# The first 26 units of a Fourier-transform and feed-forward kernel: another order of weight conversion, other engines for input folds and products

## The chip, the cores and the metric

The kernel runs on one core of a Trainium2 chip. The metric is the device time of one execution in microseconds (us). One core has five engines with an instruction stream each: TensorE (PE, matrix products; its weight loads are listed as PEld), VectorE (DVE), ScalarE (ACT), GpSimd (POOL) and SyncE (SP), which here issues the DMA transfers. Each engine takes its instructions in the order in which they are written; semaphores order the engines among each other. Data lies in SBUF (on-chip memory), results of TensorE in PSUM, which is divided into eight banks of 128 partitions x 512 float32.

## The reference

```python
X = np.fft.fft(x, axis=1)            # x: 8 x 3008 x 256 float32
X = np.fft.fft(X, axis=2)
x = X.real.astype(np.float32).reshape(24064, 256)
h = x @ w_in                         # w_in: 256 x 2048, float64
g = np.where(h >= 1, h, np.where(h <= -1, 0.0, (h + 1) ** 2 / 4))
out = (g @ w_out).astype(np.float32) # w_out: 2048 x 256, float64
```

The real part of a two-dimensional Fourier transform of each of 8 batches goes through a feed-forward layer: a product with w_in, a function that is quadratic between -1 and 1, a product with w_out.

## The kernel before

**Transform.** The sequence axis, 3008 = 47 x 64, is transformed in two stages of matrix products with small constant matrices (cs). A batch comes in 8 pieces (x_b_q, 512 KB each). A piece is *folded* (fold_x, L131: the sum y of its two halves), then multiplied (stage1_sums, L291, s1), copied into z (stage1_copy, L309), and after all 8 pieces six stage-2 sums follow (stage2_sums, L352, s2). Each s2 piece is *split* into a rounded high part pqh (ScalarE) and the rest pql (VectorE) (split, L165). Two s2 pieces make the columns of one of three chunks k. The transform along the last axis is folded into w_in: fold_w_in (L264) multiplies converted w_in by the constant matrix cm (wps) and ScalarE stores the high part wh; fold_low (L280) stores the low part wl on VectorE. One row of it is kept apart as delta (spread_delta, copy_delta, move_delta).

**Weights.** float64 is not a type of the chip, so each weight tile n (0 to 15, 128 x 512 values) is read as integer words and rebuilt as float32: convert_fields (a: mantissa and exponent, two VectorE instructions), convert_floats (b: three on ScalarE), convert_join (c: two on VectorE), convert_scale (d: the product of both on GpSimd; v: the same on VectorE). Tiles 4j and 4j+1 are quarter j of w_in, tiles 4j+2 and 4j+3 are tiles 2j and 2j+1 of w_out (wo_j holds the two).

**Feed-forward.** The work is cut into units (b, k, f): 128 of the 2048 inner columns for one chunk of one batch. Units 0 to 11 are f = 0 to 3 for k = 0, 1, 2 of batch 0; units 12 to 23 are f = 4 to 15 for k = 0. gemm1(i) (L392) makes six matmuls into two PSUM tiles uv; VectorE forms us and h (L404 to L407), ScalarE a (L410, L411). activate(i) (L414) forms g on VectorE (L419); up to unit 23 it stays float32 and gemm2(i) (L437) adds g @ w_out into four accumulators acc with unsplit w_out. In the loop over i, gemm1(i) and activate(i-1) are followed by the steps of the table, and by gemm2 of the unit i-2, from i = 14 on i-4, since gemm2 is left out at i = 8 and 13. From unit 24 on g and w_out are split in high and low parts (u and O make those of w_out) and GpSimd forms g's low part.

**Order.** What comes first is written out by hand: the string START (L67) and the table STEPS (L72) name, by a letter and a number, what is issued at the start and behind gemm1 of each unit up to 26. The letters: l a weight load, k and m the loads of cs and cm, x the load of an input piece, y and g its fold on VectorE and GpSimd, p the sums of stage 1 (p0 to p7), of the Nyquist row (p8) and of stage 2 (p9 to p14 are s2 pieces 0 to 5), z and w copies of s1 into z (z on ScalarE alone, w in halves on both), q the split of an s2 piece (q9 to q14), a b c d v the conversion, f the fold of w_in, s its low part, e and E delta, n the Nyquist row's load, u and O the split of w_out, L and Y load and fold of batch 1's pieces, i and j matmuls on constants that keep TensorE busy. pin (L538) ties every engine to this order up to unit 23.

**PSUM.** Three banks serve uv, four acc0 to acc3, one "fft". While acc is not in use yet, the transform of batch 0 takes the acc banks in turn:

```python
    def fft_bank(b, name):                              # L158
        if b == 0 and early[0] < EARLY_BANKS:
            early[0] += 1
            return ps.tile([P, CH], F32, tag=f"acc{early[0] % 4}", name=name, bufs=1)
        return ps.tile([P, CH], F32, tag="fft", name=name, bufs=1)
```

The first EARLY_BANKS requests go to the acc banks, all later ones to the one "fft" bank, where each waits until the one before it has been read.

Of the kernel before, what the change touches and what calls it, by code (L numbers as in the profile page):

```python
# [113 lines left out]
def fft_ffn_kernel(ctx: ExitStack, tc: tile.TileContext, x, cst, w_in, w_out, out):  # L114
# [16 lines left out]
    def fold_x(b, q, engine=None):  # L131

        t = xt.pop((b, q))
        y = sb.tile([96, CH], F32, tag="y", name=f"y_{b}_{q}", bufs=3)
        (engine or nc.gpsimd).tensor_tensor(y, t[:96, 0], t[:96, 1], op=ALU.add)  # L135
# [127 lines left out]

    def fold_w_in(n):  # L264
        f4, m = divmod(n, 2)
        cols = slice(f4 * CH, (f4 + 1) * CH)
# [4 lines left out]
        for h in range(2):
            nc.tensor.matmul(pt, mats[m][h], f32s[4 * f4 + h], start=(h == 0), stop=(h == 1))  # L272
        nc.scalar.activation(wh[m][:, cols], pt, AF.Copy, scale=inner if m else 1.0)
# [4 lines left out]
        folds[n] = pt

    def fold_low(n):  # L280
        f4, m = divmod(n, 2)
        cols = slice(f4 * CH, (f4 + 1) * CH)
        high = wh[m][:, cols].bitcast(F32)
        if m == 1:
            nc.vector.scalar_tensor_tensor(wl[m][:, cols], folds.pop(n), inner, high, op0=ALU.mult, op1=ALU.subtract)  # L285
# [358 lines left out]
```

## Time and profile before

| | us |
|---|---|
| median of 3 runs (1757.78 to 1761.95) | 1759.48 |
| the profiled execution | 1761.39 |
| its span in the trace | 1759.5 |
| PE busy in the span | 1736.8 |
| VectorE busy | 1427.5 |
| ScalarE busy | 1338.1 |
| GpSimd busy | 1149.9 |

The span runs from the first to the last recorded instruction of the profiled execution; some 1.9 us of its time lie around it. Busy time is the time in which an engine worked on an instruction, and the rest of the span is idle time, of which the trace says what ended it. A row of a timeline such as `36.12 3.47 PE L460 MATMUL acc<-g,wo ... x8 [1.56 <-DVE g L419]` reads: at 36.12 us TensorE began eight matmuls of line 460, which took 3.47 us together, after 1.56 us of idle time that ended when VectorE had finished g. The granted clock is the share of full speed that TensorE was given.

### The profile page before, as it was taken

The numbers are of one execution on the slowest core, as the hardware profiler recorded it, in microseconds if no ns is written. First come the engines' busy times: TensorE is split into PE (matmuls) and PEld (weight loads), VectorE is DVE, ScalarE is ACT, GpSimd is POOL, SyncE is SP. The second block draws the span as 40 slices with busy tenths as digits, with TensorE's granted clock in tenths as the row PEclk, the third lists the DMA queues.
The fourth block names the chain that finished last, engine by engine and source line by source line (L and its number), as shares of the span: only waits on it lengthen the run. The fifth ranks groups of instructions, "written<-read, shape, count | busy, mean of one in ns | idle before, by whom it ended". The sixth has DMA issues, their size and how long they took to land.

```text
span 1759.5 us, 21528 instructions
## 1 busy us (share of the span) xinstructions
PE 1736.8 (99%) x7822; PEld 1393.5 (79%) x7822; DVE 1427.5 (81%) x1753; ACT 1338.1 (76%) x1564; POOL 1149.9 (65%) x800
## 2 busy tenths in 40 slices
PE   8999999999999999999999999999999999999998
PEld 6545788888888888888888888888888878887876
DVE  6998788788887887887887788877888788888886
ACT  6776877787777777787777877778778777777775
POOL 1103757876678766677667776677667766667766
PEclk9999999999999999999999999999999999999999
DMA  8104311110011100111001100111001001000000
GB/s 313 47 24 142 107 66 60 37 60 30 1 60 51 45 30 13 60 58 33 24 13 60 59 31 25 42 42 59 19 25 37 1 24 42 1 25 19 5 24 24
DMA packets 33738, 80.89 MB, mean 46 GB/s; under 512 B 4704, under 2 KB 9952, under 8 KB 33632
## 3 DMA queue, kind: packets, MB, share of 16 engines
q1 hardware_dynamic: 33596, 79.52, 13.1%
q8 instruction: 61, 1.00, 0.2%
q14 instruction: 45, 0.37, 0.1%
q10 hardware_dynamic: 36, 0.01, 0.0%
HBM read 51.70 MB, written 27.81 MB: 45 GB/s over the span
## 4 chain that ended last, share of the span: by engine, by line
PE 56%; ACT 17%; DVE 10%; POOL 9%; issue 7%; DMA 0%; ACTq 0%; SPq 0%; POOLq 0%; DVEq 0%
PE acc L460 35%; PE uv L401 17%; POOL gl L428 8%; DVE h L422 7%; ACT a L411 6%; ACT gh L425 5%; ACT a L410 4%; PE s L298 2%; PE s L364 2%; DVE h L406 1%; DVE h L407 1%; ACT z L321 1%; DMA cm<-in_cst_dram 0%; DVE us L404 0%; PE wps L272 0%
## 5 line engine op out<-in xcount | busy, mean ns | idle before, releaser
L428 POOL TENSOR_TENSOR gl<-h,gh 128x512 fp32r<-128x512 f32 (+1 forms) x720 | 1033.6, 1458 | 447.1 <-ACT gh L425 416.8
L422 DVE SCALAR_TENSOR_TENSOR h<-a,h 128x1024 f32<-128x1024 f32 (+1 forms) x360 | 547.1, 1520 | 225.1 <-ACT a L411 223.7
L425 ACT ACTIVATE gh<-h 128x1024 fp32r<-128x1024 f32 (+1 forms) x360 | 376.7, 1046 | 347.2 <-DVE h L422 306.5
L460 PE MATMUL acc<-gh,woh 128*128 128x512 f32 (+1 forms) x1440 | 570.2, 396 | 3.6 <-DVE o L471 2.2
L460 PE MATMUL acc<-gl,woh 128*128 128x512 f32 (+1 forms) x1440 | 563.8, 392 | 0.9 <-POOL gl L428 0.9
L460 PE MATMUL acc<-gh,wol 128*128 128x512 f32 (+1 forms) x1440 | 560.8, 389 | 0.0
L410 ACT ACTIVATE a<-h,biases 128x1024 f32<-128x1024 f32 (+1 forms) x384 | 432.3, 1126 | 39.9 <-DVE h L407 38.1
L411 ACT ACTIVATE a<-a 128x1024 f32<-128x1024 f32 (+1 forms) x384 | 399.5, 1040 | 7.7
L460 PEld LDWEIGHTS acc<-gh,woh 128*128 128x128 f32 x1440 | 270.7, 188 | 62.3 <-DVE o L471 5.6
L460 PEld LDWEIGHTS acc<-gl,woh 128*128 128x128 f32 x1440 | 271.3, 188 | 58.6 <-POOL gl L428 2.2
L401 PE MATMUL uv<-pqh,wh 128*128 128x512 f32 (+1 forms) x768 | 310.6, 404 | 5.6 <-DVE h L407 2.7
L460 PEld LDWEIGHTS acc<-gh,wol 128*128 128x128 f32 x1440 | 270.7, 188 | 54.7
L406 DVE TENSOR_TENSOR h<-us,uv 128x512 f32<-128x512 f32 (+1 forms) x384 | 259.8, 677 | 62.4 <-POOL gl L428 18.8
L401 PE MATMUL uv<-pqh,wl 128*128 128x512 f32 (+1 forms) x768 | 299.5, 390 | 0.8 <-DVE wl L285 0.8
L401 PE MATMUL uv<-pql,wh 128*128 128x512 f32 (+1 forms) x768 | 299.6, 390 | 0.0
L404 DVE SCALAR_TENSOR_TENSOR us<-nyb,delta,uv 128x512 f32<-128x512 f32 (+1 forms) x384 | 279.2, 727 | 17.8 <-PE uv L401 17.2
L407 DVE TENSOR_TENSOR h<-us,uv 128x512 f32<-128x512 f32 (+1 forms) x384 | 256.4, 668 | 0.0
L401 PEld LDWEIGHTS uv<-pqh,wh 128*128 128x128 f32 x768 | 144.2, 188 | 50.1 <-DVE h L407 8.4
L401 PEld LDWEIGHTS uv<-pqh,wl 128*128 128x128 f32 x768 | 144.5, 188 | 34.2 <-issue 5.0
L401 PEld LDWEIGHTS uv<-pql,wh 128*128 128x128 f32 x768 | 144.4, 188 | 30.3 <-DVE pql L167 0.4
L135 POOL TENSOR_TENSOR y<-x 96x512 f32<-96x512 f32 x59 | 103.8, 1762 | 62.4 <-DMA x<-in_x_dram 40.7
L460 PE MATMUL acc<-g,wo 128*128 128x482 f32 (+1 forms) x192 | 86.2, 591 | 3.3 <-DVE g L419 2.3
(64 smaller groups left out, 687.4 us busy)
## 6 DMA issues: line engine op xcount, KB each, us to landing
x<-in_x_dram SPq DMA_DIRECT2D x64, 512.0 KB, 3.5
out_dram<-o SPq DMA_DIRECT2D x26, 512.0 KB, 2.8
out_dram<-o SPq DMA_DIRECT2D x14, 482.0 KB, 2.9
nyb<-nyr SPq DMA_DIRECT2D x24, 256.0 KB, 3.2
raw<-in_moe_w_in_dram SPq DMA_DIRECT2D x4, 512.0 KB, 6.7
raw<-in_moe_w_out_dram SPq DMA_DIRECT2D x4, 512.0 KB, 10.5
part<-o SPq DMA_DIRECT2D x4, 512.0 KB, 3.1
os<-part SPq DMA_DIRECT2D x4, 512.0 KB, 6.1
```

The source lines that it names most:

```text
L135: (engine or nc.gpsimd).tensor_tensor(y, t[:96, 0], t[:96, 1], op=ALU.add)
L298: nc.tensor.matmul(pt[:, i], y[:, i * P : (i + 1) * P], bm[:96, :], start=True, stop=True)
L401: nc.tensor.matmul(t[:, :n], w[m][:, cols], r[:, m, :n], start=(j == 0), stop=(j == 2))
L404: nc.vector.scalar_tensor_tensor(us, nyb[b, k][:, :n], delta[:, f : f + 1], uv[0], op0=ALU.mult, op1=ALU.add)
L406: nc.vector.tensor_tensor(h[:, 0], us, uv[1], op=ALU.subtract)
L407: nc.vector.tensor_tensor(h[:, 1], us, uv[1], op=ALU.add)
L410: nc.scalar.activation(a, h, AF.Relu, bias=half, scale=0.5)
L411: nc.scalar.activation(a, a, AF.Square)
L422: nc.vector.scalar_tensor_tensor(h, a, 1.0, h, op0=ALU.min, op1=ALU.max)
L425: nc.scalar.activation(gh, h, AF.Copy)
L428: nc.gpsimd.tensor_tensor(gl[:, sg], h[:, sg], gh[:, sg].bitcast(F32), op=ALU.subtract)
L460: nc.tensor.matmul(acc[:, :n], w, g[:, sg], start=(begin and j == 0), stop=(last and j == len(terms) - 1))
```

## The change

Eight things change:

1. **Input folds of batch 0.** Pieces 2 to 6 are folded on GpSimd, pieces 0, 1 and 7 on VectorE (before: 5, 6, 7 on GpSimd). The load of cm stands ahead of the pieces, the low parts and copies are ordered anew, and the warming matmuls at the start are 5 instead of 7.
2. **First w_in quarter.** The folds wps_0 and wps_1 are made in two halves (fold_half, step F): the first matmul of each as soon as tile 0 is converted, the second behind tile 1.
3. **delta.** Its row is taken (take_delta) behind the low part, and delta's spread (e0) stands behind the first two stage-2 sums.
4. **EARLY_BANKS** 13 becomes 12; e0 is the twelfth request, so piece 2 of stage 2 (p11) takes the "fft" bank. Wps 3 and 5 (SPARE) take uv banks as before; wps 7 takes the "fft" bank instead of a uv bank.
5. **Units 0 to 2.** activate(0) is called as G0 in step 0, ahead of gemm1(1); the split q11 moves from step 0 to step 1, q12 from step 1 to step 2.
6. **Units 12 to 26.** The last w_in quarter (tiles 12, 13) is converted ahead of the w_out tiles 7, 10 and 11; its folds f6, f7 come in steps 17 and 18. All w_out products go to GpSimd (d in place of v). Batch 1's pieces are loaded one at a time (L0 to L3), its stage-1 pieces begin at unit 23 instead of 22 (NEXT).
7. **Folds of batch 1** (Y0, Y1) wait for the last VectorE instruction issued ahead of them (fold_x_behind_vector).
8. The low parts in w_in's quarters 1 to 3 are made ahead of the row's copy.

```diff
@@ -65,14 +65,14 @@
 
 
 START = (
-    "l0 l1 k x0 x1 x2 m0 x3 x4 x5 x6 x7 l2 a0 b0 a1 b1 c0 v0 y0 p0 t0 z0 p8 n0 "
-    "l3 l4 l5 n1 n2 l8 l9 l6 l7 l12 l13 l10 l11 l14 l15 c1 v1 f0 y1 p1 z1 y2 s0 f1 p2 y3 z2 y4 p3 g5 g6 g7 s1 w3 p4 "
-    "w4 j1 p5 w5 j1 p6 a2 w6 j1 p7 e0 j1 w7 E0 p9 p10 q9 q10 b2"
+    "l0 l1 k m0 x0 x1 x2 x3 x4 x5 x6 x7 l2 l3 a0 b0 a1 b1 c0 v0 F0 F1 y0 p0 t0 j3 p8 c1 v1 w0 f0 y1 p1 g2 s0 f1 n0 "
+    "l4 l5 n1 n2 l8 l9 l6 l7 l12 l13 l10 l11 l14 l15 w1 s1 p2 g3 w2 p3 g4 w3 p4 g5 w4 p5 g6 y7 w5 j1 p6 j1 w6 p7 j2 w7 "
+    "a2 p9 p10 R0 q9 e0 q10 E0 b2"
 )
 STEPS = {
-    0: "p11 c2 d2 q11 i4",
-    1: "p12 a3 q12 b3 i4",
-    2: "a4 c3 d3 b4",
+    0: "p11 c2 d2 G0 i4",
+    1: "q11 p12 a3 b3 i4",
+    2: "a4 c3 d3 b4 q12",
     3: "c4 d4",
     4: "p13 a5 q13 b5",
     5: "p14 q14",
@@ -81,21 +81,21 @@
     8: "f2 f3 c8 d8 s2 s3 r1",
     9: "a9 b9",
     11: "a6 c9 d9 b6",
-    12: "a7 c6 d6 b7",
-    13: "f4 f5 c7 d7 s4 s5 r2",
-    14: "a12 b12 u0",
-    15: "O0 u1",
-    16: "a13 c12 v12 O1 b13",
-    17: "a10 c13 v13 b10",
-    18: "c10 v10 f6 a11 s6 b11 u2",
-    19: "f7 | c11 v11 s7 r3 O2",
-    20: "L a14 b14 u3",
-    21: "Y0 a15 c14 v14 O3 b15",
-    22: "Y1 c15 v15 u4",
-    23: "O4 u5",
-    24: "O5 u6",
-    25: "O6 u7",
-    26: "O7",
+    12: "a12 b12",
+    13: "f4 f5 c6 d6 s4 s5 r2",
+    14: "a13 c12 d12",
+    15: "b13",
+    16: "a7 c13 d13 b7",
+    17: "f6 c7 d7 s6 u0 L0 L1",
+    18: "f7 a10 s7 b10 r3 u1",
+    19: "a11 c10 d10 b11",
+    20: "a14 O0 Y0 b14 u2 L2",
+    21: "O1 c11 d11 u3",
+    22: "a15 O2 Y1 b15 L3 u4",
+    23: "O3 c14 d14 u5",
+    24: "O4 c15 d15 u6",
+    25: "O5 u7",
+    26: "O6 O7",
 }
 
 RAW = {0: "gh", 1: "gh", 2: "woh", 3: "woh", 4: "woh", 5: "woh", 6: "wol", 7: "wol", 8: "wol", 9: "wol"}
@@ -103,11 +103,12 @@
 WORK = {1: "a", 3: "a", 4: "gl", 5: "gl", 7: "a", 8: "gl", 9: "gl", 11: "a", 12: "gl", 13: "gl", 15: "a"}
 BUFS = {"h": 3, "a": 3, "gl": 4}
 
-EARLY_BANKS = 13
+EARLY_BANKS = 12
 FIRST = 4
 NATIVE = 24
 PINNED = 24
-NEXT = 22
+SPARE = (3, 5)
+NEXT = 23
 
 
 @with_exitstack
@@ -131,13 +132,20 @@
     def fold_x(b, q, engine=None):
 
         t = xt.pop((b, q))
+        engine = engine or nc.gpsimd
         y = sb.tile([96, CH], F32, tag="y", name=f"y_{b}_{q}", bufs=3)
-        (engine or nc.gpsimd).tensor_tensor(y, t[:96, 0], t[:96, 1], op=ALU.add)
+        first = engine.tensor_tensor(y, t[:96, 0], t[:96, 1], op=ALU.add)
         yt[b, q] = y
         if q == 0:
             y = sb.tile([96, NA], F32, tag="yd", name=f"yd_{b}", bufs=1)
-            nc.gpsimd.tensor_tensor(y, t[:96, 0, :NA], t[:96, 1, :NA], op=ALU.subtract)
+            engine.tensor_tensor(y, t[:96, 0, :NA], t[:96, 1, :NA], op=ALU.subtract)
             yt[b, "d"] = y
+        return first.ins
+
+    def fold_x_behind_vector(q):
+        last = [ins for ins in traced if ins.engine == mybir.EngineType.DVE][-1]
+        sync = mybir.DependencyInfo(mybir.DependencyClass.Sync, mybir.DependencyReason.DATA)
+        tc.add_manual_dep(fold_x(1, q), last.name, sync, reason="beside VectorE's next steps")
 
     cs = wts.tile([P, _OFF[2]], F32, name="cs")
     bm, rm = (cs[:, _OFF[i] : _OFF[i + 1]] for i in range(2))
@@ -261,30 +269,40 @@
                 delta[:, f4 * 4 + i : f4 * 4 + i + 1], row[:, i * P : (i + 1) * P].rearrange("o (p x) -> o p x", x=1)
             )
 
+    def fold_half(n, h):
+        f4, m = divmod(n, 2)
+        if h == 0:
+            if f4 == 0 or n in SPARE:
+                folds[n] = ps.tile([P, CH], F32, tag="uv", name=f"wps_{n}", bufs=3)
+            else:
+                folds[n] = fft_bank(f4, f"wps_{n}")
+        nc.tensor.matmul(folds[n], mats[m][h], f32s[4 * f4 + h], start=(h == 0), stop=(h == 1))
+
     def fold_w_in(n):
         f4, m = divmod(n, 2)
         cols = slice(f4 * CH, (f4 + 1) * CH)
-        if m or f4 == 0:
-            pt = ps.tile([P, CH], F32, tag="uv", name=f"wps_{n}", bufs=3)
-        else:
-            pt = fft_bank(f4, f"wps_{n}")
-        for h in range(2):
-            nc.tensor.matmul(pt, mats[m][h], f32s[4 * f4 + h], start=(h == 0), stop=(h == 1))
-        nc.scalar.activation(wh[m][:, cols], pt, AF.Copy, scale=inner if m else 1.0)
-        if m == 1:
-            row = sb.tile([1, CH], F32, tag="y" if f4 else "us", name=f"row_{f4}", bufs=3 if f4 else 2)
-            nc.scalar.activation(row, pt[0:1], AF.Copy)
-            deltas[f4] = row
-        folds[n] = pt
+        if n not in folds:
+            fold_half(n, 0)
+        fold_half(n, 1)
+        nc.scalar.activation(wh[m][:, cols], folds[n], AF.Copy, scale=inner if m else 1.0)
+
+    def take_delta(f4):
+        row = sb.tile([1, CH], F32, tag="y" if f4 else "us", name=f"row_{f4}", bufs=3 if f4 else 2)
+        nc.scalar.activation(row, folds.pop(2 * f4 + 1)[0:1], AF.Copy)
+        deltas[f4] = row
 
     def fold_low(n):
         f4, m = divmod(n, 2)
         cols = slice(f4 * CH, (f4 + 1) * CH)
         high = wh[m][:, cols].bitcast(F32)
+        pt = folds.pop(n)
         if m == 1:
-            nc.vector.scalar_tensor_tensor(wl[m][:, cols], folds.pop(n), inner, high, op0=ALU.mult, op1=ALU.subtract)
+            nc.vector.scalar_tensor_tensor(wl[m][:, cols], pt, inner, high, op0=ALU.mult, op1=ALU.subtract)
+            folds[n] = pt
+            if f4:
+                take_delta(f4)
         else:
-            nc.vector.tensor_tensor(wl[m][:, cols], folds.pop(n), high, op=ALU.subtract)
+            nc.vector.tensor_tensor(wl[m][:, cols], pt, high, op=ALU.subtract)
 
     s1, s2 = {}, {}
 
@@ -485,7 +503,7 @@
         for _ in range(n):
             nc.tensor.matmul(bank, src[:, :P], src, start=True, stop=True)
 
-    keep_warm(7, warm)
+    keep_warm(5, warm)
 
     n1 = XC
 
@@ -503,8 +521,8 @@
         "m": lambda n: nc.sync.dma_start(cm, cst[:, _OFF[2] :]),
         "x": lambda n: load_x(0, n),
         "y": lambda n: fold_x(0, n, nc.vector),
-        "L": lambda n: [load_x(1, q) for q in range(4)],
-        "Y": lambda n: fold_x(1, n),
+        "L": lambda n: load_x(1, n),
+        "Y": fold_x_behind_vector,
         "g": lambda n: fold_x(0, n),
         "p": piece_sums,
         "z": lambda n: stage1_copy(0, n),
@@ -516,7 +534,10 @@
         "c": convert_join,
         "d": lambda n: convert_scale(n, nc.gpsimd),
         "v": lambda n: convert_scale(n, nc.vector),
+        "F": lambda n: fold_half(n, 0),
         "f": fold_w_in,
+        "G": activate,
+        "R": take_delta,
         "s": fold_low,
         "u": w_out_high,
         "O": w_out_low,
@@ -561,7 +582,7 @@
             gemm1(i)
             if b == 0 and units[i][2] == NFT - 2:
                 load_parts(units[i][1])
-            if 0 < i <= PINNED:
+            if 1 < i <= PINNED:
                 activate(i - 1)
             if i >= PINNED:
                 activate(i)```

In the order below a row is line, operation, out<-in, and size; the numbers at the ends of names are buffer numbers. First VectorE, from us of unit 0 on, before:

```order
L404 SCALAR_TENSOR_TENSOR us_0_314<-nyb_0_0_152,delta_72,uv_0_0_306 128x482
L406 TENSOR_TENSOR h_0_316<-us_0_314,uv_0_1_310 128x482
L407 TENSOR_TENSOR h_0_316<-us_0_314,uv_0_1_310 128x482
L213 SCALAR_TENSOR_TENSOR cv_2_261<-raw_woh_112,cv_2_261 128x512
L214 SCALAR_TENSOR_TENSOR cv_2_261<-raw_woh_112,cv_2_261 128x512
L167 TENSOR_TENSOR pql_0_1_323<-s2_0_2_324,pqh_0_1_322 128x4x2x64
L404 SCALAR_TENSOR_TENSOR us_1_348<-nyb_0_0_152,delta_72,uv_1_0_340 128x482
L406 TENSOR_TENSOR h_1_350<-us_1_348,uv_1_1_344 128x482
L407 TENSOR_TENSOR h_1_350<-us_1_348,uv_1_1_344 128x482
L419 SCALAR_TENSOR_TENSOR g_0_356<-a_0_319,h_0_316 128x2x482
```

and the same place now:

```order
L422 SCALAR_TENSOR_TENSOR us_0_315<-nyb_0_0_176,delta_72,uv_0_0_307 128x482
L424 TENSOR_TENSOR h_0_317<-us_0_315,uv_0_1_311 128x482
L425 TENSOR_TENSOR h_0_317<-us_0_315,uv_0_1_311 128x482
L221 SCALAR_TENSOR_TENSOR cv_2_277<-raw_woh_110,cv_2_277 128x512
L222 SCALAR_TENSOR_TENSOR cv_2_277<-raw_woh_110,cv_2_277 128x512
L437 SCALAR_TENSOR_TENSOR g_0_334<-a_0_320,h_0_317 128x2x482
L422 SCALAR_TENSOR_TENSOR us_1_349<-nyb_0_0_176,delta_72,uv_1_0_341 128x482
L424 TENSOR_TENSOR h_1_351<-us_1_349,uv_1_1_345 128x482
L425 TENSOR_TENSOR h_1_351<-us_1_349,uv_1_1_345 128x482
L175 TENSOR_TENSOR pql_0_1_324<-s2_0_2_325,pqh_0_1_323 128x4x2x64
```

The low half pql of stage-2 piece 2 and g of unit 0 have changed places around unit 1's us and h.

Then TensorE at the sums of stage-2 piece 3, between gemm1(1) and gemm1(2), with the semaphores that a row waits for, before:

```order
L401 MATMUL uv_1_1_344<-pql_0_0_288,wh1_69 128x482
L364 MATMUL s2_0_3_358<-cs_66,z_0_133 128x128 x4
L486 MATMUL warm_bank_371<-cs_66 128x128 [waits PE_49]
L486 MATMUL warm_bank_371<-cs_66 128x128 x3
L401 MATMUL uv_2_0_376<-pqh_0_0_287,wh0_68 128x482 [waits DVE_49]
```

and now:

```order
L419 MATMUL uv_1_1_345<-pql_0_0_281,wh1_69 128x482
L382 MATMUL s2_0_3_359<-cs_66,z_0_136 128x128 [waits DVE_49,PE_49]
L382 MATMUL s2_0_3_359<-cs_66,z_0_136 128x128 x3
L504 MATMUL warm_bank_370<-cs_66 128x128 [waits PE_49]
L504 MATMUL warm_bank_370<-cs_66 128x128 x3
L419 MATMUL uv_2_0_375<-pqh_0_0_280,wh0_68 128x482
```

The sums of piece 3, which waited for nothing, wait for VectorE now: for the pql of piece 2 that stands last in the VectorE rows above.

Last GpSimd, from the second half of wo_1 to the folds of batch 1, before:

```order
L228 TENSOR_TENSOR wo_1_728<-cv_6_692 128x512
L228 TENSOR_TENSOR wo_1_728<-cv_7_723 128x512
L135 TENSOR_TENSOR y_1_0_1036<-x_1_0_999 96x512
L139 TENSOR_TENSOR yd_1_1038<-x_1_0_999 96x64
L135 TENSOR_TENSOR y_1_1_1077<-x_1_1_1001 96x512
L135 TENSOR_TENSOR y_1_2_1122<-x_1_2_1003 96x512
L135 TENSOR_TENSOR y_1_3_1189<-x_1_3_1005 96x512
```

and now:

```order
L236 TENSOR_TENSOR cv_13_790<-cv_13_790 128x512
L236 TENSOR_TENSOR wo_1_758<-cv_7_857 128x512
L236 TENSOR_TENSOR wo_2_969<-cv_10_928 128x512
L137 TENSOR_TENSOR y_1_0_1001<-x_1_0_898 96x512
L141 TENSOR_TENSOR yd_1_1003<-x_1_0_898 96x64
L236 TENSOR_TENSOR wo_2_969<-cv_11_964 128x512
L137 TENSOR_TENSOR y_1_1_1068<-x_1_1_900 96x512
L137 TENSOR_TENSOR y_1_2_1148<-x_1_2_1009 96x512
L137 TENSOR_TENSOR y_1_3_1217<-x_1_3_1073 96x512
L236 TENSOR_TENSOR wo_3_1101<-cv_14_996 128x512
L137 TENSOR_TENSOR y_1_4_1288<-x_1_4_1117 96x512
L236 TENSOR_TENSOR wo_3_1101<-cv_15_1064 128x512
```

The products of tiles 10, 11, 14 and 15 have come to GpSimd from VectorE, and lie between the folds of batch 1; those of tiles 12 and 13 stand ahead of tile 7's.

## The prediction

> **What bounds the kernel now.** I read the shares of busy time first, then the span in windows, then TensorE's own timeline. In the quoted rows of the timeline the columns are start, duration, engine, line, operation and, in brackets, the idle time ahead of the row with what ended it; in the windows they are the stretch, its length, the busy time of PE, PEld, DVE, ACT and POOL with counts, the granted clock, the DMA share and GB/s.
>
> ```profile
> PE 1736.8 (99%) x7822; PEld 1393.5 (79%) x7822; DVE 1427.5 (81%) x1753; ACT 1338.1 (76%) x1564; POOL 1149.9 (65%) x800
> 0.00:100.00 100.00, 94.70 (x364) 57.59 (x365) 79.99 (x135) 68.13 (x104) 15.47 (x17) 1.00 0.43 159
> 100.00:200.00 100.00, 94.19 (x334) 59.48 (x333) 87.52 (x120) 71.22 (x100) 32.37 (x25) 0.97 0.32 110
> 300.00:500.00 200.00, 200.00 (x930) 166.44 (x929) 164.18 (x195) 156.47 (x180) 146.53 (x100) 1.00 0.10 34
> ```
>
> TensorE is busy without a gap from 300 us on, and nothing behind unit 41 changes its order there. So the change can move the end only through what TensorE loses in the first 200 us: a microsecond saved or lost there shifts all that follows. VectorE has little room (87.52 of 100 in the second window). The losses there are these:
>
> ```profile
> 26.26 0.49 PE L401 MATMUL uv<-pqh,wh 128*128 128x482 f32 x1 [0.69 <-ACT pqh L166]
> ...
> 36.12 3.47 PE L460 MATMUL acc<-g,wo 128*128 128x482 f32 x8 [1.56 <-DVE g L419]
> ...
> 130.74 0.49 PE L401 MATMUL uv<-pqh,wh 128*128 128x482 f32 x1 [1.85 <-ACT wh L273]
> 131.99 0.77 PE L401 MATMUL uv<-pqh,wl 128*128 128x482 f32 x1 [0.76 <-DVE wl L285]
> ...
> 153.79 1.10 PE L298 MATMUL s<-cs,y 96*128 96x96 f32 x8 [1.52 <-issue]
> 130.00:140.00 10.00, 8.50 (x21) 4.87 (x22) 7.80 (x14) 5.65 (x9) 0.88 (x1) 0.83 0.52 179
> 150.00:160.00 10.00, 8.48 (x26) 4.89 (x25) 9.86 (x14) 8.18 (x18) 1.43 (x1) 0.83 0.34 105
> ```
>
> The first unit's product starts at 26.26 us. Four waits follow, and two of them (1.85 with 0.76, and 1.52) are followed by ten microseconds at a mean clock of 0.83: 0.17 x 10 = 1.7 us of TensorE work lost behind each. The wait of 1.56 at 36 us drew no such dip (1.00 over the first window).
>
> **Term 1, the start: -1.5 us.**
>
> ```profile
> 17.33 3.72 POOL L135 TENSOR_TENSOR y<-x 96x512 f32<-96x512 f32 x3 [7.89 <-PE s L298]
> ...
> 21.36 1.03 PE L298 MATMUL s<-cs,y 96*128 96x96 f32 x8
> L128 SPq DMA_DIRECT2D x<-in_x_dram x8: 328/432/607, 2.1 to 9.8; - x8
> DMA to landing us min/median/max: 8.9/9.4/9.8
> ...
> L135 DVE TENSOR_TENSOR y<-x 96x512 f32<-96x512 f32 x5 | 3.2, 680 | 0.2 <-DMA x<-in_x_dram 0.2
> ```
>
> Before, GpSimd makes the last three input folds one after the other (17.33 to 21.05), and the sums of pieces 6 and 7 start at 21.36, 4.9 us ahead of 26.26. After, GpSimd folds pieces 2 to 6 as they land and VectorE folds 0, 1 and 7. The last piece is issued at 9.8 and lands 8.9 to 9.8 later, at 18.7 to 19.6, and its fold is 0.68 on VectorE: the sums can start at 19.4 to 20.3 instead of 21.36, 1.1 to 2.0 us earlier. The 4.9 behind it stay about as they were: six more copies of 0.36 lie on VectorE, which the folds given to GpSimd make room for, and delta's matmuls move behind the two stage-2 sums. On SP the load of the fold matrices moves ahead of the pieces; the conversion of the first weights hides it. I take 1.5; 2.5 if delta's move counts in full, 0 if the copies on VectorE end last.
>
> **Term 2, units 0 to 2: +5.4 us, and +1.7 for the clock.** EARLY_BANKS falls from 13 to 12, and delta's spread, twelfth now, takes the last early bank. The sums of stage-2 piece 2 then go to the single "fft" bank, and those of piece 3, next in it, must wait until piece 2 is split (pqh on ScalarE, pql on VectorE). Before, they were in two banks. The split itself moves from step 0 to step 1, so on ScalarE it now stands behind unit 1's activations.
>
> ```profile
> 29.67 0.46 PE L401 MATMUL uv<-pqh,wh 128*128 128x482 f32 x1
> ...
> 31.08 1.05 PE L364 MATMUL s<-cs,z 128*128 128x128 f32 x8
> ...
> 32.78 0.47 PE L401 MATMUL uv<-pqh,wh 128*128 128x482 f32 x1
> ...
> 30.73 1.01 ACT L411 ACTIVATE a<-a 128x964 f32<-128x964 f32 x1
> ...
> 34.99 1.10 ACT L410 ACTIVATE a<-h,biases 128x964 f32<-128x964 f32 x1 [2.77 <-DVE h L407]
> ...
> 37.04 0.58 ACT L166 ACTIVATE pqh<-s 128x512 fp32r<-128x512 f32 x1
> ...
> 37.65 0.69 DVE L167 TENSOR_TENSOR pql<-s,pqh 128x512 fp32r<-128x512 f32 x1 [1.01 <-ACT pqh L166]
> ```
>
> Counted from gemm1(0) (26.26): a of unit 0 ends at 31.74, +5.5, and g of unit 0, now ahead of us of unit 1, takes about the 1.1 us that pql had kept VectorE from it, so a of unit 1 still starts at +8.7 (34.99) and its second pass ends at +10.8 (37.04). There the split of piece 2 runs where before that of piece 3 ran: pqh 0.58, then pql from +11.4 (37.65) to +12.1. Piece 3's sums, which started at +4.8 (31.08), start at **+12.1**: TensorE, which works in order, stands for 7.1 us. Behind it come these sums and the keep-warm matmuls (31.08 to 32.78, 1.7), gemm1(2) (29.67 to 31.08, 1.41), and gemm2(0) at +15.2. Before it began at 36.12, +9.86. The loss is 5.4, not 7.3, because the wait of 1.56 and smaller ones on VectorE are absorbed. TensorE has no idle time behind it in which to catch up (94.70 busy in the first window, whose first 26 us are the start). With 7.1 us of standing the clock surely drops, as it did behind 1.85: 1.7 more (0.9 if a wait on the next g swallows half of it, 2.5 if the dip lasts half as long again). That G0 lets g be early buys nothing, since gemm2(0) stands behind piece 3's sums.
>
> The Trainium skill, "TensorE: Matmul & The Clock Gate", section "HAM oscillation — how this bites in real kernels", has a rule of "no PE-idle gaps >~3.4µs". By that rule the new wait of 7.1 us draws a dip, and waits of 1 to 2 us, such as the change brings at units 20 to 24 (below), never do: the time would be the forecast's, and the slower rival R1 would fall away. The trace disagrees, since the waits of 1.85 and of 1.52 us were each followed by a stretch at 0.83; I go by the rows and keep R1.
>
> **Term 3, units 16 to 25: -5.5 us.**
>
> ```profile
> 67.74 3.60 PE L272 MATMUL wps<-cv,cm 128*128 128x512 f32 x8
> 70.77 0.80 PE L401 MATMUL uv<-pqh,wh 128*128 128x512 f32 x1
> ...
> 104.74 0.78 PE L401 MATMUL uv<-pqh,wh 128*128 128x482 f32 x1
> ...
> 136.80 0.76 PE L401 MATMUL uv<-pqh,wh 128*128 128x482 f32 x1
> ...
> 138.49 3.40 PE L460 MATMUL acc<-g,wo 128*128 128x482 f32 x8
> 141.34 0.76 PE L401 MATMUL uv<-pqh,wh 128*128 128x482 f32 x1
> ...
> 146.26 1.03 PE L298 MATMUL s<-cs,y 96*128 96x96 f32 x8
> ...
> 147.47 0.48 PE L401 MATMUL uv<-pqh,wh 128*128 128x482 f32 x1
> ...
> 160.64 0.77 PE L401 MATMUL uv<-pqh,wh 128*128 128x512 f32 x1
> ```
>
> From gemm1(16) (104.74) to gemm1(25) (160.64) TensorE takes 55.9 us. The work in it is nine units of 4.54 (136.80 to 141.34), two weight folds of 3.03 together (67.74 to 70.77), and batch 1's first sums, 1.21 and 1.10: 46.2. So 9.7 us are lost there: the waits for the last w_in quarter (1.85, 0.76), 1.52, two dips of 1.7, and about 2 in small pieces. After, that quarter is converted ahead of two w_out tiles, its high part follows directly on ScalarE and its low part stands ahead of us of unit 19, so these waits and their dips go. What is late next is w_out, whose products all go to GpSimd:
>
> ```profile
> 92.78 0.71 DVE L404 SCALAR_TENSOR_TENSOR us<-nyb,delta,uv 128x482 f32<-128x482 f32 x1
> ...
> 90.91 0.42 DVE L200 TENSOR_SCALAR cv<-raw_wol 128x512 uint32<-128x512 uint32 x1
> ...
> 97.18 1.27 POOL L228 TENSOR_TENSOR wo<-cv 128x512 f32<-128x512 f32 x1 [2.87 <-DVE cv L214]
> ...
> 138.03 0.72 DVE L404 SCALAR_TENSOR_TENSOR us<-nyb,delta,uv 128x482 f32<-128x482 f32 x1 [1.04 <-PE uv L401]
> ```
>
> gemm2(16) needs tile 10. Its joins stand behind us, h, h and g on VectorE in step 19, as those did that ended in the product at 97.18: from us (92.78) to its end (98.45) are 5.67 us. Here two field instructions of 0.42, which overlap a little, 0.7 together, stand in between, and us starts 1.23 behind gemm1 (136.80 to 138.03) and some 0.25 later behind the low part: 1.23 + 0.25 + 5.67 + 0.7 = 7.8 us behind gemm1(19). TensorE has gemm1(19), gemm2(15) and gemm1(20) until then, 1.69 + 2.85 + 1.69 = 6.2: a wait of **1.6**. gemm2(18) on tile 11 waits in the same way, a little less, 1.3. gemm2(20) on tile 14 waits 1.0, or 2.0 if the fold of piece 1_3, queued ahead of the product on GpSimd and waiting for batch 1's first sums, holds it. Small ones (gemm2(14) on tile 7, the bank at unit 16) are 0.3 together. So 9.7 - 4.2 = 5.5 is won. Six products of 0.69 leave VectorE; that is what pays for g, not more. Bounds: 3 (waits of 2.0 where I take 1.0, and one dip) to 7.5 (the waits halved).
>
> The folds of batch 1 are tied to VectorE's last step so as to lie beside its steps from PSUM. Why that might matter:
>
> ```profile
> 141.55 2.88 POOL L135 TENSOR_TENSOR y<-x 96x512 f32<-96x512 f32 x2
> ...
> 141.79 1.52 DVE L201 TENSOR_SCALAR cv<-raw 128x512 uint32<-128x512 uint32 x1
> ```
>
> While GpSimd folded, a field instruction took 1.52 us against 0.42. Better placing is worth at most some 1.1 us per fold on VectorE, and lies in the 9.7 above. SP's loads of batch 1 become four single ones, the first behind tile 7's join, not later than the folds need them, and the batch's pieces start one unit later, which the room behind 200 us takes up.
>
> **Sum.** -1.5 + 5.4 + 1.7 - 5.5 = +0.1 on the profiled execution, 1761.39 us (its span of 1759.5 and 1.9 around it), which is 1.9 above the median. So 1759.5 against the median: **no change**, its own range 1756 to 1763.
>
> **Rivals.**
> R1, slower: the waits for GpSimd's products at gemm2(16) and (18) draw the half clock as 1.85 and 1.52 did. It decides at a wait between 1.52 and 1.56, since 1.56 drew none once and 1.52 did: 1.6 and 1.3 stand at that point. Two dips give back 3.4 of the 5.5, and the early dip's upper bound adds 0.8: 1759.5 + 4.2, near 1763.7. For it: every long wait behind 130 us drew one. Against: the one at 36 us did not.
> R2, faster: GpSimd's products keep up, because VectorE, freed of six products, reaches its joins earlier than my chain says: the 4.2 of new waits go, 1755.3. For it: VectorE waits 1.04 for uv at 138.03, so it is ahead there; against: GpSimd's product is 1.27 against 0.69 and is the last link.
> R3, the ties do not do what they say: the folds and products run beside VectorE's SBUF steps all the same. Two instructions stretched as at 141.79 cost 2.2: 1761.7.
>
> **Chances.** Forecast 0.50, R1 0.24, R2 0.18, R3 0.08. A measurement of this kernel tells about 0.2%, 3.5 us, from no change. The forecast's edges give 0.04 to faster, and with R3's upper half 0.03 to slower: faster 0.22, same 0.51, slower 0.27. The range takes in R1's and R2's centres with the early dip's bound: 1754.0 to 1764.5.
>
> **What would show it.** Right: gemm1(0) at 24.3 to 25.2; a wait of about 7 us ahead of piece 3's sums, ended by pql, and a low clock in the windows behind it; gemm2(0) 15 us behind gemm1(0); no waits on wh or wl near unit 19, but waits of 1 to 2 us for wo on GpSimd ahead of three gemm2. Wrong: if piece 3's sums wait under 3 us the kernel is faster than I say; if dips follow the product waits, slower.

## The result, and the profile after

The changed kernel is slower: 1769.28 us against 1758.78, ratio 1.0055 [1.0038, 1.0073], outside the forecast range (1754.0 to 1764.5). In a later series it took 1777.53 (experiment 5). The two profiled executions below lie only 6.2 us apart, because that of before is 2.6 above its median and that of the changed kernel 1.7 below.

| | before | after |
|---|---|---|
| profiled execution, its span (us) | 1761.39, 1759.5 | 1767.59, 1765.8 |
| gemm1(0) starts | 26.26 | 27.57 |
| gemm2(0) starts | 36.12 | 45.52 |
| gemm1(16) starts | 104.74 | 113.29 |
| gemm1(27) starts | 170.79 | 177.88 |
| gemm1(44) starts | 252.38 | 259.90 |

TensorE's timeline of the changed kernel at its waits, and its windows, columns as above:

```profile
15.85 1.10 PE L316 MATMUL s<-cs,y 96*128 96x96 f32 x8 [2.15 <-DVE y L137]
...
27.57 0.49 PE L419 MATMUL uv<-pqh,wh 128*128 128x482 f32 x1
...
39.88 2.04 PE L382 MATMUL s<-cs,z 128*128 128x128 f32 x8 [7.56 <-DVE pql L175]
...
45.52 3.40 PE L478 MATMUL acc<-g,wo 128*128 128x482 f32 x8
...
139.26 5.20 PE L478 MATMUL acc<-g,wo 128*128 128x482 f32 x8 [2.04 <-POOL wo L236]
151.47 3.50 PE L478 MATMUL acc<-g,wo 128*128 128x482 f32 x8 [1.16 <-POOL wo L236]
164.10 1.08 PE L478 MATMUL acc<-g,wo 128*128 128x482 f32 x2 [1.64 <-POOL wo L236]
```

```profile
10.00:20.00 10.00, 7.85 (x53) 5.99 (x52) 5.72 (x12) 3.94 (x12) 4.96 (x4) 1.00 0.97 378
30.00:40.00 10.00, 2.44 (x16) 1.93 (x15) 6.13 (x11) 4.71 (x5) 1.27 (x1) 0.74 0.94 360
40.00:50.00 10.00, 10.00 (x36) 7.78 (x37) 5.30 (x10) 4.90 (x7) 0.00 (x0) 0.74 0.01 6
140.00:150.00 10.00, 10.00 (x27) 5.34 (x25) 6.80 (x12) 6.86 (x9) 1.54 (x2) 0.83 0.50 168
```

The wait ahead of stage-2 piece 3 is there, 7.56 us, ended by pql as foretold. Work behind it ran at a mean clock of 0.74 from 40 to 50 us: 0.26 x 10 = 2.6 us lost. The waits on wh and wl are gone; in their place stand three on GpSimd's wo, the first with a dip (a short stretch at half clock) behind it. New is the wait of 2.15 at 15.85, in the start.

### The profile page after: what moved, and what is told of

Its sections match the earlier page's. It is cut to its first block, busy times and chain, and to the rows that moved or that the text cites. A ratio compares the mean times of both kernels' runs of the same rounds, so it can differ in the third digit from the quotient of the medians.

```text
span 1765.8 us, 21536 instructions
## 1 busy us (share of the span) xinstructions
PE 1735.6 (98%) x7824; PEld 1394.4 (79%) x7824; DVE 1421.5 (80%) x1752; ACT 1334.8 (76%) x1558; POOL 1164.2 (66%) x807
## 4 chain that ended last, share of the span: by engine, by line
PE 53%; ACT 15%; POOL 12%; DVE 10%; issue 9%; DMA 0%; ACTq 0%; POOLq 0%; SPq 0%; DVEq 0%
PE acc L478 33%; PE uv L419 16%; POOL gl L446 12%; DVE h L440 6%; ACT a L429 5%; ACT gh L443 4%; ACT a L428 4%; PE s L316 2%; PE s L382 1%; PE wps L279 1%; DVE h L424 1%; DVE h L425 1%; ACT z L339 1%; POOL y L137 0%; DVE us L422 0%
## 5 line engine op out<-in xcount | busy, mean ns | idle before, releaser
L478 PE MATMUL acc<-gh,woh 128*128 128x512 f32 (+1 forms) x1440 | 570.5, 396 | 3.9 <-DVE o L489 2.5
L478 PE MATMUL acc<-gl,woh 128*128 128x512 f32 (+1 forms) x1440 | 563.9, 392 | 1.3 <-POOL gl L446 1.3
L478 PE MATMUL acc<-gh,wol 128*128 128x512 f32 (+1 forms) x1440 | 560.9, 390 | 0.0
L478 PEld LDWEIGHTS acc<-gh,woh 128*128 128x128 f32 x1440 | 270.7, 188 | 62.8 <-DVE o L489 5.9
L478 PEld LDWEIGHTS acc<-gl,woh 128*128 128x128 f32 x1440 | 271.3, 188 | 58.9 <-POOL gl L446 2.6
L478 PEld LDWEIGHTS acc<-gh,wol 128*128 128x128 f32 x1440 | 270.8, 188 | 54.7
L419 PE MATMUL uv<-pqh,wh 128*128 128x512 f32 (+1 forms) x768 | 310.7, 405 | 1.3 <-DVE h L425 1.0
L424 DVE TENSOR_TENSOR h<-us,uv 128x512 f32<-128x512 f32 (+1 forms) x384 | 259.7, 676 | 62.7 <-POOL gl L446 19.9
L422 DVE SCALAR_TENSOR_TENSOR us<-nyb,delta,uv 128x512 f32<-128x512 f32 (+1 forms) x384 | 279.1, 727 | 30.5 <-PE uv L419 29.9
L419 PE MATMUL uv<-pqh,wl 128*128 128x512 f32 (+1 forms) x768 | 299.6, 390 | 0.0
L419 PE MATMUL uv<-pql,wh 128*128 128x512 f32 (+1 forms) x768 | 299.2, 390 | 0.0
L425 DVE TENSOR_TENSOR h<-us,uv 128x512 f32<-128x512 f32 (+1 forms) x384 | 256.2, 667 | 0.0
L419 PEld LDWEIGHTS uv<-pqh,wh 128*128 128x128 f32 x768 | 144.6, 188 | 45.1 <-DVE h L425 6.7
L419 PEld LDWEIGHTS uv<-pqh,wl 128*128 128x128 f32 x768 | 144.5, 188 | 33.5 <-issue 5.3
L419 PEld LDWEIGHTS uv<-pql,wh 128*128 128x128 f32 x768 | 144.3, 188 | 30.4 <-issue 0.2
L137 POOL TENSOR_TENSOR y<-x 96x512 f32<-96x512 f32 x61 | 107.2, 1759 | 28.1 <-DMA x<-in_x_dram 10.2
L478 PE MATMUL acc<-g,wo 128*128 128x482 f32 (+1 forms) x192 | 85.9, 590 | 5.6 <-POOL wo L236 4.8
```

Of the source, the lines that this page charges most:

```text
L137: first = engine.tensor_tensor(y, t[:96, 0], t[:96, 1], op=ALU.add)
L419: nc.tensor.matmul(t[:, :n], w[m][:, cols], r[:, m, :n], start=(j == 0), stop=(j == 2))
L422: nc.vector.scalar_tensor_tensor(us, nyb[b, k][:, :n], delta[:, f : f + 1], uv[0], op0=ALU.mult, op1=ALU.add)
L424: nc.vector.tensor_tensor(h[:, 0], us, uv[1], op=ALU.subtract)
L425: nc.vector.tensor_tensor(h[:, 1], us, uv[1], op=ALU.add)
L478: nc.tensor.matmul(acc[:, :n], w, g[:, sg], start=(begin and j == 0), stop=(last and j == len(terms) - 1))
```

## The experiments

The experiments were measured in three series, each with its own runs of the kernel before, whose medians were 1760.57 (1 to 4), 1759.88 (5 to 8) and 1760.10 us (9 to 12, on another chip).

| | median us (lowest to highest) | ratio to before |
|---|---|---|
| 1 before again | 1763.47, one run | |
| 2 early part undone | 1766.63 (1758.64 to 1773.03) | 1.0030 [1.0012, 1.0048] |
| 3 start undone | 1768.20 (1765.85 to 1769.03) | 1.0044 [1.0032, 1.0056] |
| 4 late part alone | 1759.78 (1757.21 to 1761.98) | 0.9998 [0.9989, 1.0007] |
| 5 changed kernel again | 1777.53 (1776.67 to 1779.28) | 1.0093 [1.0080, 1.0106] |
| 6 EARLY_BANKS 13 | 1765.66 (1762.12 to 1775.22) | 1.0033 [1.0018, 1.0048] |
| 7 split in step 0 | 1764.67 (1761.10 to 1773.71) | 1.0024 [1.0011, 1.0037] |
| 8 fold of piece 1 first | 1758.13 (1754.85 to 1761.66) | 0.9986 [0.9976, 0.9995] |
| 9 products on VectorE | 1753.66 (1752.44 to 1755.23) | 0.9961 [0.9948, 0.9973] |
| 10 folds untied | 1757.06 (1754.53 to 1758.88) | 0.9980 [0.9971, 0.9989] |
| 11 joins first | 1754.38 (1753.87 to 1757.22) | 0.9968 [0.9956, 0.9979] |
| 12 both | 1752.61 (1752.03 to 1753.46) | 0.9956 [0.9943, 0.9968] |

**1. The kernel before, unchanged.**

> The kernel before once more, for a second trace. Theory T (the windows of the half clock run freely, so a wait of 1.5 to 1.9 us draws a dip in some executions and not in others): about 1758.8 us, the waits of 1.85 and 0.76 on wh and wl and of 1.52 ahead of batch 1's second sums again, but not both dips in the same places. Rival (a dip is fixed to these waits): both dips again, 1761 us.

The two stretches that held the dips, and TensorE's longest wait in each:

```profile
130.00:140.00 10.00, 7.55 (x22) 4.28 (x23) 8.83 (x15) 5.77 (x9) 1.39 (x2) 1.00 0.44 145
150.00:160.00 10.00, 7.38 (x23) 4.73 (x22) 9.19 (x13) 8.81 (x17) 1.71 (x1) 0.83 0.24 75
```

```profile
131.68 0.48 PE L401 MATMUL uv<-pqh,wh 128*128 128x482 f32 x1 [1.84 <-ACT wh L273]
...
154.44 1.44 PE L298 MATMUL s<-cs,y 96*128 96x96 f32 x8 [2.62 <-issue]
```

The wait on wh is the same, 1.84, and no dip follows it (1.00; before, 1.85 and 0.83). So the dips are not fixed to the waits, as T has it. The wait ahead of batch 1's second sums is not the same, 2.62 for 1.52, and has its dip again. The time of 1763.47 was higher than T's, and one run can't say more.

**2. The changed kernel with the early part undone.**

```diff
-    0: "p11 c2 d2 G0 i4",  1: "q11 p12 a3 b3 i4",  2: "a4 c3 d3 b4 q12",
+    0: "p11 c2 d2 q11 i4", 1: "p12 a3 q12 b3 i4",  2: "a4 c3 d3 b4",
-EARLY_BANKS = 12
+EARLY_BANKS = 13
-            if 1 < i <= PINNED:
+            if 0 < i <= PINNED:
```

> The changed kernel with EARLY_BANKS 13 and steps 0 to 2 of before (q11 in step 0, q12 in step 1, g of unit 0 behind gemm1(1)). Theory T (the wait of 7.56 us ahead of stage-2 piece 3, with its half clock, is most of the loss): 8 to 9 us faster than the changed kernel, 1760 to 1761.5 us; the wait is gone and gemm2(0) starts 9.9 us behind gemm1(0). Rival U (the loss lies at GpSimd's products behind unit 16): 1764 us or more.

The 7.56 us wait is gone, and the lowest runs (1758.64 to 1760.33) lie at before's level. But most lie higher, up to 1773, and the median of 1766.63 is not T's. The profiled execution (1767.10) was one of these; its windows in the start:

```profile
10.00:20.00 10.00, 7.85 (x41) 5.84 (x41) 5.53 (x11) 3.21 (x10) 3.79 (x3) 0.86 0.98 386
20.00:30.00 10.00, 10.00 (x48) 9.88 (x47) 4.88 (x13) 3.98 (x12) 2.52 (x2) 0.50 0.97 335
30.00:40.00 10.00, 9.99 (x58) 9.22 (x58) 5.34 (x10) 5.65 (x9) 0.56 (x1) 0.79 0.95 362
```

TensorE ran at half clock from about 17 to 34 us, and gemm1(0) began at 35.02. Neither theory had this.

**3. The changed kernel with the start of before** (its START, seven warming matmuls, delta's row behind wh).

> The changed kernel with the start of before (input folds, copies, warming and delta in the old order; the rest as changed). Theory T (the new start brings gemm1(0) 1.3 us later, 27.57 against 26.26): gemm1(0) at 26.3, 1768 us, 1.3 less than the changed kernel. By the prediction's first term it would be 1.5 slower than the changed kernel, 1770.8.

gemm1(0) at 26.61, no low clock ahead of it, 1768.20: T's numbers. What is left of the change costs 7.6 us (1768.20 - 1760.57).

**4. The kernel before, with only the late part of the change** (steps 12 to 26, loads and ties of batch 1, products on GpSimd, the bank of wps 7, item 8).

> The kernel before up to unit 11, and only the new steps 12 to 26, loads and folds of batch 1, and the products on GpSimd. Theory T (the trace of the changed kernel shows 1.5 us won from gemm1(16) to unit 27): 1757 us. By the prediction's third term: 1753.3. Rival U (the new waits for GpSimd's products cost more than the old waits): 1761 or more.

No difference: neither the 5.5 us of the third term nor U's loss, nor T's 1757. The three waits on wo are in its trace (2.02, 1.16, 1.65), and two dips (0.83 from 130 to 140 and from 180 to 190 us). The kernel of experiment 3 has the early part besides and takes 8.4 us more (1768.20 - 1759.78): that is the early part.

**5. The changed kernel again.**

> The changed kernel once more, beside the next three. Theory T: about 9 us slower than before, 1769. If TensorE's wait of 2.15 us ahead of the sums of piece 1 draws the half clock in some executions, as in the trace of the run without the early change (half clock from 17.2 to 34.2 us, gemm1(0) at 35.0), single runs lie some 7 us higher, near 1776; the rival (the low clock there came from something else in that kernel) has none above 1772.

TensorE's timeline and one window of the start:

```profile
15.89 1.99 PE L316 MATMUL s<-cs,y 96*128 96x96 f32 x8 [2.15 <-DVE y L137]
...
36.56 0.48 PE L419 MATMUL uv<-pqh,wh 128*128 128x482 f32 x1
```

```profile
20.00:30.00 10.00, 10.00 (x49) 10.00 (x48) 5.04 (x12) 4.30 (x13) 2.54 (x2) 0.50 1.02 333
```

All five runs lie between 1776.67 and 1779.28. The wait of 2.15 is as long as in the first trace; there the clock stayed at 1.00, here it fell to 0.50, and gemm1(0) came 9 us later (36.56 against 27.57).

**6. EARLY_BANKS 13 alone; 7. the split back in step 0 alone.**

```diff
-EARLY_BANKS = 12
+EARLY_BANKS = 13
```

> The changed kernel with EARLY_BANKS 13 alone: stage-2 piece 2 takes an acc bank again, its split stays in step 1. Theory B (the bank makes the wait): piece 3's sums wait for nothing; what is late then is gemm2(0), whose second accumulator waits for the split of piece 2, 12.1 us behind gemm1(0); runs without a low clock at the start 6 us faster than the changed kernel, 1763. Rival O (the order on ScalarE and VectorE makes the loss, whatever the bank): 1767 or more.

```diff
-    0: "p11 c2 d2 G0 i4",      1: "q11 p12 a3 b3 i4",
+    0: "p11 c2 d2 q11 G0 i4",  1: "p12 a3 b3 i4",
```

> The changed kernel with the split of stage-2 piece 2 (q11) back in step 0, ahead of g of unit 0; EARLY_BANKS stays 12. Theory P (it takes both, the shared bank and the late split): piece 3's sums wait 2 us instead of 7.5, gemm2(0) starts 10 to 11 us behind gemm1(0), 1761 to 1762 in runs without a low clock at the start. If the bank alone were the cause: the wait stays above 5 us and 1767 or more.

TensorE in 6, then in 7:

```profile
47.27 4.39 PE L478 MATMUL acc<-g,wo 128*128 128x482 f32 x6 [3.04 <-DVE pql L175]
```

```profile
34.11 1.32 PE L382 MATMUL s<-cs,z 128*128 128x128 f32 x8 [1.84 <-DVE pql L175]
```

With the old bank piece 3 waits for nothing and gemm2(0) waits 3.04 for the late split; with the early split the shared bank costs 1.84. The lowest runs are 1762.1 and 1761.1. It takes both to make 7.56, as B and P say of their halves; the bank alone is not the cause, nor the order alone. Their higher runs are above what the waits explain; in 6 the profiled execution was one of them, with gemm1(0) at 35.10, the start's low clock again. In 7 it was not, so for 7 that is not shown.

**8. As 2, with the fold of piece 1 ahead of the copies of piece 0.** On VectorE of the changed kernel the fold stands behind a copy that waits for ScalarE, whose own stands behind the issue of a transfer (VectorE, then ScalarE). Before, ScalarE made these copies alone and the fold started at 11.24 (last row):

```profile
14.25 0.73 DVE L337 COPY z<-s 64x192 f32<-64x192 f32 x2 [2.67 <-ACT z L339]
15.02 0.69 DVE L137 TENSOR_TENSOR y<-x 96x512 f32<-96x512 f32 x1
```

```profile
12.93 0.56 ACTq L360 DMA_DIRECT2D nyr<-nyt  x1
13.54 0.68 ACT L339 ACTIVATE z<-s 64x192 f32<-64x192 f32 x2 [0.64 <-ACT nyt L357]
```

```profile
11.24 1.28 DVE L135 TENSOR_TENSOR y<-x 96x512 f32<-96x512 f32 x2
```

```diff
-    ... p8 c1 v1 w0 f0 y1 p1 ...
+    ... p8 c1 v1 y1 w0 f0 p1 ...
```

> As the run with the early change undone (new start, new late part, EARLY_BANKS and steps 0 to 2 of before), and in the start the fold of piece 1 ahead of the copies of piece 0 on VectorE. Theory S (VectorE's copies wait for ScalarE's, behind the Nyquist row and its transfer's issue, and hold the fold of piece 1; TensorE then stands 2.15 us, which draws the low clock): the wait ahead of piece 1's sums falls under 1 us, gemm1(0) starts at 25.5 to 26.5, all runs between 1757 and 1762, median 1759. Rival W (five warming matmuls instead of seven make the low clock): the runs still spread over 10 us or more.

```profile
13.43 1.10 PE L316 MATMUL s<-cs,y 96*128 96x96 f32 x8
...
25.24 0.48 PE L419 MATMUL uv<-pqh,wh 128*128 128x482 f32 x1
```

The wait is gone, gemm1(0) starts at 25.24, and twelve runs lie within 7 us, none at the upper level, still with five warming matmuls: S, not W. This version is faster than before by its interval.

**9 to 12, all on the kernel of 8.** 9: the products of tiles 10, 11, 14 and 15 on VectorE.

```diff
-    19: "a11 c10 d10 b11",
+    19: "a11 c10 v10 b11",
-    21: "O1 c11 d11 u3",
+    21: "O1 c11 v11 u3",
-    23: "O3 c14 d14 u5",
+    23: "O3 c14 v14 u5",
-    24: "O4 c15 d15 u6",
+    24: "O4 c15 v15 u6",
```

> As the run with the fold of piece 1 first (1758.1 us), and the products of w_out tiles 10, 11, 14 and 15 on VectorE again. Theory G (GpSimd's product, 1.27 us, is the last link of the waits of 2.05, 1.16 and 1.63): each of them falls by some 0.6, the kernel by 1.5 to 2, 1756.5. Rival V (VectorE, with 2.8 us more work, passes the delay on to us of the next unit): no gain, 1758 or more.

10: batch 1's folds untied.

```diff
-        "Y": fold_x_behind_vector,
+        "Y": lambda n: fold_x(1, n),
```

> As the run with the fold of piece 1 first, with batch 1's folds no longer tied to VectorE's steps. Theory N (where these folds lie decides nothing that TensorE waits for): 1758, the same. Rival C (untied they lie beside VectorE's SBUF steps and stretch them, as a field instruction of 1.52 against 0.42 in the kernel before): 1 to 2 us slower, with field or join instructions over 1 us on VectorE.

11: the joins first in their steps.

```diff
-    19: "a11 c10 d10 b11",
+    19: "c10 d10 a11 b11",
-    21: "O1 c11 d11 u3",
+    21: "c11 d11 O1 u3",
-    23: "O3 c14 d14 u5",
+    23: "c14 d14 O3 u5",
-    24: "O4 c15 d15 u6",
+    24: "c15 d15 O4 u6",
```

> As the run with the fold of piece 1 first, with the joins of tiles 10, 11, 14 and 15 ahead of the field or low-part instructions in their steps (GpSimd still makes the products). Theory G: the waits fall by 0.7 each where VectorE's queue is what is late, 2.05 to 1.35, 1.16 to 0.5; 1756.5. Rival D (the half clock, not the waits, is the loss, and falls as before): 1758.

12: 9 and 11 together.

> The last change and the products on VectorE together. Theory G: waits of 0.7, 0 and 0.3, too short for a half clock behind them: 3.5 us and one dip of 1.7 less than with the fold of piece 1 first, 1753 to 1754.6. Rival D or V: 1757 to 1758.

TensorE's waits for wo in 8, 9, 11 and 12, in this order:

```profile
129.04 3.50 PE L478 MATMUL acc<-g,wo 128*128 128x482 f32 x8 [2.05 <-POOL wo L236]
139.56 3.50 PE L478 MATMUL acc<-g,wo 128*128 128x482 f32 x8 [1.15 <-POOL wo L236]
...
152.17 1.07 PE L478 MATMUL acc<-g,wo 128*128 128x482 f32 x2 [1.63 <-POOL wo L236]
```

```profile
128.63 3.50 PE L478 MATMUL acc<-g,wo 128*128 128x482 f32 x8 [1.41 <-DVE wo L236]
138.54 3.50 PE L478 MATMUL acc<-g,wo 128*128 128x482 f32 x8 [0.54 <-DVE wo L236]
```

```profile
128.44 3.50 PE L478 MATMUL acc<-g,wo 128*128 128x482 f32 x8 [1.40 <-POOL wo L236]
138.97 3.50 PE L478 MATMUL acc<-g,wo 128*128 128x482 f32 x8 [1.18 <-POOL wo L236]
...
151.14 1.07 PE L478 MATMUL acc<-g,wo 128*128 128x482 f32 x2 [1.41 <-POOL wo L236]
```

```profile
129.11 3.50 PE L478 MATMUL acc<-g,wo 128*128 128x482 f32 x8 [0.74 <-DVE wo L236]
139.04 3.50 PE L478 MATMUL acc<-g,wo 128*128 128x482 f32 x8 [0.57 <-DVE wo L236]
```

GpSimd's product is a link of all three waits: with VectorE's (9) they fall by 0.64, 0.61 and all of 1.63, 2.9 together. The join's place (11) counts at the first, 0.65, and hardly at the others, against G: 0.8 together. In 12 they fall by 3.5, and in their place stands one of 0.59 on us (151.08). The medians fall by more, 4.5, 3.8 and 5.5 (from 1758.13, in the series before), and part of that is dips: the profiled execution of 8 had two dips (0.83 in the windows from 30 to 40 and from 180 to 190 us), that of 9 one, those of 11 and 12 none, at 1.7 each. One execution each is no measure of how often a dip comes. Rival D, which had the dips fall as before, is out with that, and rival V falls by the time.

Untying the folds (10) changes nothing that the intervals can tell, though the third wait is 1.24 there for 1.63. Beside GpSimd's folds VectorE's instructions stretch either way, in 8 a join (0.68 alone), in 10 a field instruction (0.42 alone):

```profile
148.99 1.78 DVE L222 SCALAR_TENSOR_TENSOR cv<-raw,cv 128x512 uint32<-128x512 uint32 x1
```

```profile
143.62 1.50 DVE L208 TENSOR_SCALAR cv<-raw 128x512 uint32<-128x512 uint32 x1
```

## Why the prediction was wrong, step by step

**Term 1, -1.5, failed in its mechanism.** The step "six more copies of 0.36 lie on VectorE, which the folds given to GpSimd make room for" counted their length and not what they wait for. The first pair stood 2.67 us for ScalarE, with the fold of piece 1 behind it: that came at 15.02, the folds behind it later in turn, and gemm1(0) at 27.57. With that fold moved the gain is there: 25.24 in 8 and 25.29 to 25.48 in 9 to 11, against 26.26 to 27.26 in four traces with the old start. Only 12 has 26.61, behind a wait of 1.17 for the load of cm, which "the conversion of the first weights hides it" took for hidden. The wait of 2.15 that the late fold makes is also what the low clock of the start hangs on, some 9 us where it strikes: no run of 8 to 12, which are without it, lies at that level. The forecast's bounds for this term, 0 to 2.5 gained, had no room for it; the lower one names the copies on VectorE, but at nothing gained.

**Term 2, +5.4 and +1.7, held.** Foretold were 7.1 us of standing, measured 7.56; piece 3's sums at +12.1, measured +12.3 (39.88 - 27.57); gemm2(0) at +16.9 with the clock's share, measured +17.95, so 8.1 lost for 7.1. The clock took 2.6, just over its upper bound. That both the bank and the order are needed is shown by 6 and 7.

**Term 3, -5.5, was mis-sized to nothing (experiment 4).** Its 9.7 us of loss were a difference of sums; the waits and dips in that stretch make 8.3 (1.85, 0.76, 1.52, two of 1.7, and 0.8 for an output's bank), so 1.4 of it was work. Both dips were taken as lost each time; the trace of experiment 1 has one. Of the new waits the first was 2.04 for 1.6, the third 1.64 for 1.0. VectorE's timeline of the changed kernel shows why:

```profile
132.10 0.75 DVE L300 SCALAR_TENSOR_TENSOR wl<-wps,biases,wh 128x512 fp32r<-128x512 f32 x1 [2.08 <-ACT wh L287]
132.77 0.71 DVE L422 SCALAR_TENSOR_TENSOR us<-nyb,delta,uv 128x482 f32<-128x482 f32 x1
...
160.92 1.77 DVE L222 SCALAR_TENSOR_TENSOR cv<-raw,cv 128x512 uint32<-128x512 uint32 x1
```

The low part waited 2.08 for wh, so us of unit 19 came 1.99 behind gemm1(19) (130.78), not 1.48. The join ahead of the third product took 1.77 for 0.68 beside GpSimd's fold of piece 1_3 (160.52 to 162.15), which the change does not tie: R3's stretching, on this wait. The three make 4.84, where I had 3.9 and 0.3 for small ones, and a dip followed the first: R1's mechanism, with one dip for its two. R1's point "between 1.52 and 1.56" is none, since 1.57 drew a dip in 8 and 1.84 none in 1. Behind unit 27 the changed kernel loses 0.4 more (7.09 us late at unit 27, 7.52 at unit 44): a wait ahead of later sums of batch 1, whose pieces start one unit later, is 1.45 (192.81) for 0.87, and the forecast put that shift at nothing. So from unit 16 (8.55 late) to unit 44 the trace won 1.0 of the 5.5, and experiment 4 nothing that its interval can tell. That GpSimd's product is a link of the waits is shown by 9 (2.9 of 4.8 us); that it alone makes this term nothing is not, since dips go with it. Whether batch 1's folds were tied or not (R3) decided nothing in time.

The sum in the first series: about +8 for the early part (7.1 foretold), 0 for the late one (-5.5), and +1 to +2 for the start (-1.5); in the second another 8 for the low clock. These come from medians of different series, to some 2 us. Why one series had it in no run and the next in all five is open.

The row behind "busy without a gap from 300 us on" ends at 500. From 500 to 1740 us TensorE stands 6.5 us in all in the kernel before, 7.3 in experiment 1 and 4.7 to 6.4 in the kernels with the new late part, so single executions drift apart there by one or two microseconds.

## What to carry to other kernels

When work is given to another engine (here half of the copies to VectorE), read what it waits for there and what stands behind it in that queue, not only its length. A buffer turned from several to one is harmless only until something reads it late: check the two together. Where TensorE's clock depends on its idle time, count a new wait of about 2 us at its length, and a dip as a chance (a wait of 2.04 drew one in the changed kernel, one of 2.05 in 8 none), and take away short links (a product on a slower engine, a join behind work that nobody waits for) first.

## What the runs showed of the hardware

The half clock does not belong to a wait. The same wait ahead of gemm2(0) (1.56 to 1.57 us) drew none in the kernel before and in 10, 11 and 12 but did in 8 and 9. The 2.15 to 2.16 us in the start drew it in the traces of 2, 5 and 6 and not in those of the changed kernel and of 7.

What decides is, in the main, where a wait falls. The traces also record when the granted clock changes. In each of the twelve traces with a dip all changes lie on a grid of 3.413 us, and a stretch at half clock lasts one, two, three, five or six such steps. Cut along its grid, the wait of 1.57 (33.36 to 34.93) lies in one step in 8; in 10 (33.59 to 35.16) the step's edge at 34.27 cuts it in two:

```profile
32.32:35.73 3.41, 1.83 (x6) 0.97 (x6) 3.03 (x6) 1.90 (x2) 0.00 (x0) 1.00 1.04 390
35.73:39.15 3.42, 3.42 (x6) 1.39 (x5) 2.56 (x5) 2.55 (x5) 0.00 (x0) 0.50 0.76 277
```

```profile
30.85:34.27 3.42, 2.73 (x17) 1.85 (x15) 2.87 (x5) 0.65 (x2) 0.36 (x1) 1.00 1.03 407
34.27:37.68 3.41, 2.52 (x7) 1.27 (x8) 2.40 (x5) 3.38 (x5) 0.00 (x0) 1.00 1.05 388
37.68:41.09 3.41, 2.86 (x11) 1.68 (x10) 3.27 (x7) 2.48 (x4) 0.00 (x0) 1.00 0.52 194
```

In 8 TensorE was busy for 1.83 of 3.41, 54%, and the next step came at half clock; in 10 for 80% and 74%, and the clock stayed. In the start the wait of 2.15 left 50% of a step in 5 (12.03 to 15.44) and the clock fell, 57% in the changed kernel's first trace (14.40 to 17.81), where it stayed. Over these traces all 24 drops ahead of the kernel's end follow a step in which TensorE was busy for 58% or less; of 871 steps at full clock up to 270 us that were followed by another, only 10 lie that low. So by these rows some 1.4 us of idle time within one step (0.42 x 3.41) puts the clock at risk. Busy time is modelled in the trace, so the edge is no sharper than that.

The Trainium skill, "TensorE: Matmul & The Clock Gate", section "What's actually happening", has the clock decided in windows of 3413 ns that run on whatever the kernel does; the grid of these traces agrees. The limit of 3.4 us for a gap that the same page of the Trainium skill gives in section "HAM oscillation — how this bites in real kernels" does not: gaps of 1.57, 2.04 and 2.15 us drew it. Once down in the start of 5, with TensorE listed as fully busy from 20 to 30 us (10.00 of 10.00), the clock still stayed at 0.50 for all of these ten microseconds; behind the later waits it was back after the first step in which TensorE was busy for 86% or more. Why the start differs is open.
